# Fused attention and two MoE layers on one core: both halves of a batch's q product in one burst, and the token softmax emitted by stage for both halves

## The chip, the cores and the metric

The kernel runs on one core of a Trainium2 chip. The metric is the device time of one execution in microseconds; the kernel before takes 607.36 us in the median of three runs (606.77 to 608.14).

## The reference

Three layers follow one another on 8 batches of 576 tokens with 8 heads of 64.

```python
p_packed = sm_attn(p, k, v)            # 32 packed queries per head attend to k, v
out = sm_attn(q, p_packed, p_packed)   # the tokens attend to the packed result

# MoE 1: every token goes to the one expert with the largest logit
h = np.maximum(xe @ w1[e], 0.0)
out[mask] = gate_w[mask, None] * (h @ w2[e])

# MoE 2: only tokens with a positive skip score, the others pass through
y[mask] = gate_w[mask, None] * (h @ w2[e])
out[do_compute] = xc + y
```

## The kernel before, in words

**Tiling.** The tokens of one batch are handled in two halves of 288 columns (`hf`), over 128 partitions. The first softmax (packed queries against k) gives per batch a packed matrix `PKT` (128x128). The token softmax gives, per batch, an attention matrix `A2` (128 partitions, 2 x 576) of weights on the packed rows. Since MoE 1 multiplies attention output by `w1`, the kernel does not form the attention output: it multiplies `PKT` by the batch's `w1` once (the q product, matrix Q1 of 128 x 2 x 1024) and then Q1 by `A2`. Expert weights are chosen at run time, per batch, from a register (`e1`).

**Precision.** An f32 product that must be exact to nearly full f32 is made of three fp32r matmuls, from a high part and a remainder of each operand. `split` (L596) makes them: a copy on ScalarE gives the high part (`Q1h`, `W2h`, `A2h`), a subtraction on VectorE or GpSimd gives the rest (`Q1l`, `W2l`, `A2l`). The q product itself is a plain f32 product on a tiled array (64 rows x 32 columns, helper `heads`, L384), and the trace has 16 matmul records for one half of it, and 32 for both.

**Main stream.** `gen_M(b)` is what TensorE does for batch b: for each half of the tokens `stage1` (8 steps of 6 matmuls, L690, `h`, evacuated by ScalarE L695 to `hh` and by VectorE L696 to `hl`) and `stage2` (4 output tiles t of 24 matmuls each, L711, `y`, reading `W2h`/`W2l` of t; each is multiplied by the gate on VectorE, L731). That makes 48 steps per batch. I write M(0) to M(7) for the batches' streams. After M(7) come the expert items of MoE 2.

**Side work.** `Weave` puts steps of other generators between the 48 steps, at fractional positions given in a table (L1330 on). For batch b the sides are the tail of batch b-1 (logits, gate), the attention work A (for batch b+1: token softmax `gen_T`, for b+2: first softmax `gen_S`, then the routing `gen_R`), `gen_pre(b+1)` (load `W1c`, split `A2`, q product, split Q1, load the gate row gB) and `gen_w2(b+1)` (load the four `W2c` tiles, split them: W2h on ScalarE, W2l on GpSimd). The recorded program is then put in order engine by engine by a scheduler that goes by priorities, and `tc.issue_after` adds an edge to that order on one engine.

**The places the change touches.** `gen_T` (L505 to L544): for each half two transposes into `T` (L520), a maximum (L523), subtraction (L525), exponential on ScalarE (L528), sum (L531), reciprocal (L533, L535), product with the reciprocal on GpSimd (L536), and two transposes into `A2` (L541). On TensorE 16 matmuls read the result: `L<-A,gs` (L554). `gen_pre` (L602 to L661): the two halves n of the q product, each with its own burst on TensorE, two `Q1h` casts and two `Q1l` subtractions; the `W1c` pool has two buffers, so the second half's two loads of 512 KB wait until the first burst has read the first half's. All DMAs of this part are issued in order by one queue, SP's. A `W2h`/`W2l` tile has one buffer for each t, so the cast for the next batch waits until the current batch's `y` matmuls of that t are done; the `W2c` pool has two buffers, so the third load waits until GpSimd has split the first.

Of the kernel before, what the change touches and what calls it, by code (L numbers as in the profile page):

```python
# [9 lines left out]
F32 = mybir.dt.float32  # L10
# [109 lines left out]
def attn_moe_kernel(ctx, tc, q, k, v, p, wg, w11, w12, w21, w22, out):  # L120
# [357 lines left out]
    def gen_T(b):  # L478
# [36 lines left out]
        for hf in range(2):  # L515
            T = Tt[hf]
            Tv = T.rearrange("p x (c e) -> p (x c) e", e=32)
            with tc.issue_after(d["turned"] if hf else e1_ins) if b == 0 else nullcontext():
                for x in range(2):
                    nc.vector.transpose(out=T[:, x, :], in_=s2[hf][x][:, 0:HALF])  # L520
            yield
            mx2 = st_p.tile([128, 18], F32, name="mx2")
            nc.vector.tensor_reduce(out=mx2, in_=Tv, op=ALU.max, axis=AX.X)  # L523
            yield
            (nc.gpsimd if b == 0 and hf else nc.vector).tensor_tensor(  # L525
                out=Tv, in0=Tv, in1=mx2.unsqueeze(2).to_broadcast([128, 18, 32]), op=ALU.subtract
            )
            nc.scalar.activation(out=T, in_=T, func=ACTF.Exp, scale=0.125)  # L528
            yield
            sm2 = st_p.tile([128, 18], F32, name="sm2")  # L530
            nc.vector.tensor_reduce(out=sm2, in_=Tv, op=ALU.add, axis=AX.X)  # L531
            yield
            nc.vector.tensor_scalar(out=sm2, in0=sm2, scalar1=EPS, scalar2=None, op0=ALU.add)  # L533
            rc2 = st_p.tile([128, 18], F32, name="rc2")
            nc.vector.reciprocal(out=rc2, in_=sm2)  # L535
            (nc.gpsimd if b or hf else nc.vector).tensor_tensor(  # L536
                out=Tv, in0=Tv, in1=rc2.unsqueeze(2).to_broadcast([128, 18, 32]), op=ALU.mult
            )
            yield
            for x in range(2):  # L540
                last = nc.vector.transpose(out=A2[:, x, hf * HALF:(hf + 1) * HALF], in_=T[:, x, :]).ins  # L541
            d["turned"] = last
            yield
# [57 lines left out]
    def gen_pre(b):  # L601
# [7 lines left out]
        def lw(n):  # L609
            for z in range(2):  # L610
                if b == 0 and n:
                    w = us[0]["y"].rearrange("p t c -> p (t c)")[:, F * z:F * (z + 1)]
                    w = w.rearrange("p (h f) -> p h f", h=2)
                else:
                    w = wcp.tile([128, 2, 512], F32, tag="W1c", name="W1c")
                nc.sync.dma_start(
                    out=w,
                    in_=w11[dsn(e1, 1), n, z].rearrange("o p h f -> p (o h) f"),
                )
                W1.append(w)  # L620

        lw(0)
        if b == 0:
            lw(1)
# [12 lines left out]
        for n in range(2):  # L637
            if b or n == 0:
                cuts = halve(n)
            yield TE  # L640
            ps = [mt("q1") for _ in range(2)]
            heads(ps, PKT, lambda hp: W1[2 * n + hp // 2][:, hp % 2, :], start=True, stop=True)
            if n == 0 and b:
                lw(1)
            sl = slice(512 * n, 512 * n + 512)
            for x in range(2):
                with ExitStack() as order:
                    for ins in cuts if b == 0 and n == 0 else ():
                        order.enter_context(tc.issue_after(ins))
                    split(Q1h[:, x, sl], Q1l[:, x, sl], ps[x], nc.vector)  # L650
                yield
        if b == 0:
# [66 lines left out]
    def gen_M(b, halves=(0, 1)):  # L719
        d = us[b]  # L720
        if halves[0] == 0 and "y" not in d:
            d["y"] = bulk.tile([128, 4, S], F32, tag="y", name="y1", bufs=2)
# [587 lines left out]
    for b in range(B):  # L1310
# [19 lines left out]
        if b + 1 < B:  # L1330
# [3 lines left out]
            sides.append((pre, 7, 0.66, 0.97))  # L1334
# [55 lines left out]
        elif b == B - 1:  # L1390
            us[b]["y"] = bulk.tile([128, 4, S], F32, tag="y", name="y1", bufs=2)
# [261 lines left out]
```

## Time and profile before

| | |
|---|---|
| median of 3 runs | 607.36 us (606.77 to 608.14) |
| profiled execution, time | 607.03 us |
| its span, first to last instruction | 605.4 us (1.63 us lie around it) |
| mean granted TensorE clock | 0.997 |
| busy: TensorE | 588.2 us (97%) |
| busy: VectorE | 335.7 us (55%) |
| busy: ScalarE | 211.2 us (35%) |
| busy: GpSimd | 136.5 us (23%) |
| HBM traffic | 200 GB/s over the span |
| steady batch, start of the first stage 2 to the next | 48.74 us (94.27 to 143.01) |

A busy share of 97% does not say that the matmuls run back to back at their best rate: matmuls are pipelined, their ends are modelled, and a matmul that starts late or a change between forms of matmul is counted as busy. So the rows of TensorE are to be read by their starts: in a row of `y` matmuls one starts every 0.13 us, and each larger distance is time that something cost. The chain of waits gives, in order of time, what each stretch went to; the timeline gives starts, durations and, in square brackets, the idle time before an instruction and what ended it.

### The profile page before, as it was taken

To read this page: it belongs to the slowest core of one execution; us is meant where nothing else is said; L and a number is where in the kernel's file an instruction comes from. 1 tells how busy PE (TensorE), PEld (TensorE's weight loads), DVE (VectorE), ACT (ScalarE), POOL (GpSimd) and SP (SyncE) were. 2 spreads that over 40 slices of the span, in tenths; PEclk is the share of its full clock that TensorE was granted. 3 is DMA by queue.
4 is the path that set the end of the run, shared out by engine and by line. 5 is a ranking of instruction groups with operands and counts; after the bars stand their busy time and mean duration, and the time that the engine had idled before them with its cause. 6 is when DMAs were issued, how large, how long until landed. Compare 5 with 4: busy or idle time off the path is not lost.

```text
span 605.4 us, 14688 instructions
## 1 busy us (share of the span) xinstructions
PE 588.2 (97%) x5901; PEld 528.1 (87%) x5902; DVE 335.7 (55%) x1000; ACT 211.2 (35%) x463; POOL 136.5 (23%) x122
## 2 busy tenths in 40 slices
PE   7899999999999999999999999999999999999996
PEld 3379889899889889989989988899899999998795
DVE  3878557737737746855774873445746236162110
ACT  3463441542352343244154224215324225043110
POOL 4041331050160141133114104120300230140032
PEclk9999999999999999999999999999999999999998
DMA  8887877477477476637326314969328491732064
GB/s 321 348 324 270 324 265 257 143 284 251 154 249 271 180 241 255 245 108 292 142 104 254 143 45 149 290 188 390 134 92 306 64 375 62 217 76 88 1 98 61
DMA packets 35994, 122.00 MB, mean 202 GB/s; under 512 B 5696, under 2 KB 15680, under 8 KB 29888
## 3 DMA queue, kind: packets, MB, share of 16 engines
q1 hardware_dynamic: 30352, 114.75, 51.8%
q0 software_dynamic: 3968, 4.85, 6.3%
q10 hardware_dynamic: 1584, 1.25, 0.7%
q8 instruction: 50, 0.82, 0.6%
q14 instruction: 40, 0.33, 0.2%
HBM read 91.57 MB, written 29.26 MB: 200 GB/s over the span
## 4 chain that ended last, share of the span: by engine, by line
PE 72%; DMA 7%; another core or an unknown queue 6%; issue 4%; DVE 4%; SPq 3%; ACT 2%; POOL 1%; POOLq 0%; ACTq 0%; DVEq 0%
PE y L711 28%; PE h L690 24%; PE y L1288 8%; PE s L386 3%; PE q L386 2%; DMA out_dram<-iXR 2%; PE L L554 1%; DMA W2c<-in_w_dram 1%; DMA W1c<-in_w_dram 1%; PE L L757 1%; DMA eX<-x2d 1%; PE pv L448 1%; SPq L995 1%; PE at L435 1%
## 5 line engine op out<-in xcount | busy, mean ns | idle before, releaser
L711 PE MATMUL y<-hh,W2h 128*128 128x288 f32 x512 | 156.0, 305 | 0.5 <-ACT hh L695 0.5
L711 PE MATMUL y<-hl,W2h 128*128 128x288 f32 x512 | 151.4, 296 | 0.7 <-DVE hl L696 0.6
L711 PE MATMUL y<-hh,W2l 128*128 128x288 f32 x512 | 151.2, 295 | 0.0
L711 PEld LDWEIGHTS y<-hh,W2h 128*128 128x128 f32 x512 | 96.0, 188 | 15.9 <-issue 11.9
L711 PEld LDWEIGHTS y<-hh,W2l 128*128 128x128 f32 x512 | 96.5, 188 | 1.1 <-issue 1.1
L711 PEld LDWEIGHTS y<-hl,W2h 128*128 128x128 f32 x512 | 96.2, 188 | 1.2 <-DVE hl L696 1.2
L598 POOL TENSOR_TENSOR W2l<-W2c,W2h 128x1024 fp32r<-128x1024 f32 x28 | 67.2, 2399 | 131.3 <-ACT W2h L597 72.0
L690 PE MATMUL h<-A2h,Q1h 128*128 128x288 f32 x256 | 78.0, 305 | 1.7 <-DVE T L520 1.4
L695 ACT ACTIVATE hh<-h 128x288 fp32r<-128x288 f32 x128 | 51.6, 414 | 69.9 <-PE h L690 56.9
L690 PE MATMUL h<-A2h,Q1l 128*128 128x288 f32 x256 | 75.6, 296 | 0.1
L690 PE MATMUL h<-A2l,Q1h 128*128 128x288 f32 x256 | 75.4, 295 | 0.0
L696 DVE SCALAR_TENSOR_TENSOR hl<-h,hh 128x288 fp32r<-128x288 f32 x128 | 56.5, 452 | 28.4 <-ACT hh L695 26.7
L690 PE MATMUL h<-eXh,eW1h 128*128 128x288 f32 x192 | 57.7, 301 | 0.8 <-DMA x2d<-y 0.8
L1288 PE MATMUL y<-ihh,iW2h 128*128 128x288 f32 x192 | 56.9, 296 | 0.0
L1288 PE MATMUL y<-ihh,iW2l 128*128 128x288 f32 x192 | 56.6, 295 | 0.0
L690 PE MATMUL h<-eXl,eW1h 128*128 128x288 f32 x192 | 56.6, 295 | 0.0
L1288 PE MATMUL y<-ihl,iW2h 128*128 128x288 f32 x192 | 56.6, 295 | 0.0
L690 PE MATMUL h<-eXh,eW1l 128*128 128x288 f32 x192 | 56.6, 295 | 0.0
L690 PEld LDWEIGHTS h<-A2h,Q1h 128*128 128x128 f32 x256 | 48.0, 188 | 6.0 <-issue 2.6
L731 DVE TENSOR_TENSOR y<-y,gB 128x288 f32<-128x288 f32 x60 | 26.7, 447 | 46.8 <-PE y L711 46.8
L690 PEld LDWEIGHTS h<-A2h,Q1l 128*128 128x128 f32 x256 | 48.1, 188 | 0.5 <-DVE Q1l L598 0.3
L690 PEld LDWEIGHTS h<-A2l,Q1h 128*128 128x128 f32 x256 | 48.1, 188 | 0.0
(299 smaller groups left out, 945.3 us busy)
## 6 DMA issues: line engine op xcount, KB each, us to landing
eW<-in_w_dram SPq DMA_DIRECT2D x8, 2048.0 KB
W1c<-in_w_dram SPq DMA_DIRECT2D x30, 512.0 KB
W2c<-in_w_dram SPq DMA_DIRECT2D x30, 512.0 KB
kT<-in_k_dram SPq DMA_DIRECT2D x7, 1152.0 KB
qT<-in_q_dram SPq DMA_DIRECT2D x7, 1152.0 KB
v<-in_v_dram SPq DMA_DIRECT2D x7, 1152.0 KB
x2d<-y SPq DMA_DIRECT2D x7, 1152.0 KB
out_dram<-y SPq DMA_DIRECT2D x7, 1152.0 KB
```

What stands on the lines that cost most here:

```text
L386: m = nc.tensor.matmul(out=out[x][32 * hp:32 * hp + 32], lhsT=lhsT[64 * x:64 * x + 64, 32 * hp:32 * hp + 32], rhs=rhs(hp)[64 * x:64 * x + ...
L435: last = nc.tensor.transpose(ats[x][:, 128 * j:128 * j + 128], a1[:, x, 128 * j:128 * j + 128], ident).ins
L448: nc.tensor.matmul(out=pv[x][32 * hp:32 * hp + 32], lhsT=aT[:, 4 * x + j, 32 * hp:32 * hp + 32], rhs=vm[:, 2 * hp + x, j, :], start=(j == ...
L554: nc.tensor.matmul(out=L[32 * i:32 * i + 32, 0:LN], lhsT=gs[:, g, :], rhs=A2[:, g, c:c + LN], start=(g == 0), stop=(g == 1),)
L598: z = eng.tensor_tensor(out=lo, in0=x, in1=hi.bitcast(F32), op=ALU.subtract)
L690: nc.tensor.matmul(out=ps[:, 0:nr], lhsT=l[:, t, 128 * f:128 * f + 128], rhs=r[:, t, :], start=(n == 0), stop=(n == 3 * kt - 1),)
L695: nc.scalar.activation(out=hh[:, f, :], in_=ps[:, 0:n_], func=ACTF.Relu)
L696: nc.vector.scalar_tensor_tensor(out=hl[:, f, :], in0=ps[:, 0:n_], scalar=0.0, in1=hh[:, f, :].bitcast(F32), op0=ALU.max, op1=ALU.subtract,)
L711: nc.tensor.matmul(out=ps[:, 0:HALF], lhsT=l[:, f, :], rhs=r[:, f, :], start=(n == 0), stop=(n == 23))
L731: nc.vector.tensor_tensor(out=y1[:, t, cols], in0=ps[:, 0:HALF], in1=d["gB"][:, cols], op=ALU.mult)
L757: nc.tensor.matmul(out=L[32 * i:32 * i + 32, 0:LN], lhsT=wgB[:, t, :], rhs=y1[:, t, LC[i]:LC[i] + LN], start=(t == 0), stop=(t == 3),)
L1288: nc.tensor.matmul(out=ps[:, 0:HALF], lhsT=l[:, f, 128 * t:128 * t + 128], rhs=r[:, f, c], start=(n == 0), stop=(n == 23))
```

## The change

It has two parts.

1. **One burst.** In `gen_pre(b)` for b from 1 to 7 both halves of `W1c` are loaded at once: the second half goes into the `y` buffer of the coming batch, which nothing uses yet. Both halves of `A2` are split ahead of the product, and the 32 matmuls of both q halves are emitted together, into four PSUM banks, where the second burst stood (24 `y` matmuls before the end of the batch). The four `Q1h` casts and four `Q1l` subtractions follow together. The positions in the table change to match.
2. **By stage.** In `gen_T(b)` for b from 1 to 7 the six stages (turn, most, less, total, over, back) are emitted for half 0 and half 1 in turn, with an order edge from one stage to the next up to the fourth. Batch 0 keeps its order.

The work is the same: TensorE has the same number of instructions in both.

```diff
@@ -512,35 +512,57 @@
         A2 = pk_p.tile([128, 2, S], F32, name="A2")
         d["A2"] = A2
         yield
-        for hf in range(2):
-            T = Tt[hf]
-            Tv = T.rearrange("p x (c e) -> p (x c) e", e=32)
-            with tc.issue_after(d["turned"] if hf else e1_ins) if b == 0 else nullcontext():
-                for x in range(2):
-                    nc.vector.transpose(out=T[:, x, :], in_=s2[hf][x][:, 0:HALF])
-            yield
-            mx2 = st_p.tile([128, 18], F32, name="mx2")
-            nc.vector.tensor_reduce(out=mx2, in_=Tv, op=ALU.max, axis=AX.X)
-            yield
-            (nc.gpsimd if b == 0 and hf else nc.vector).tensor_tensor(
-                out=Tv, in0=Tv, in1=mx2.unsqueeze(2).to_broadcast([128, 18, 32]), op=ALU.subtract
-            )
-            nc.scalar.activation(out=T, in_=T, func=ACTF.Exp, scale=0.125)
-            yield
-            sm2 = st_p.tile([128, 18], F32, name="sm2")
-            nc.vector.tensor_reduce(out=sm2, in_=Tv, op=ALU.add, axis=AX.X)
-            yield
-            nc.vector.tensor_scalar(out=sm2, in0=sm2, scalar1=EPS, scalar2=None, op0=ALU.add)
-            rc2 = st_p.tile([128, 18], F32, name="rc2")
-            nc.vector.reciprocal(out=rc2, in_=sm2)
-            (nc.gpsimd if b or hf else nc.vector).tensor_tensor(
-                out=Tv, in0=Tv, in1=rc2.unsqueeze(2).to_broadcast([128, 18, 32]), op=ALU.mult
-            )
-            yield
+        mxs, sms, rcs = ([st_p.tile([128, 18], F32, name=n) for _ in range(2)] for n in ("mx2", "sm2", "rc2"))
+        Tv = [T.rearrange("p x (c e) -> p (x c) e", e=32) for T in Tt]
+
+        def wide(t):
+            return t.unsqueeze(2).to_broadcast([128, 18, 32])
+
+        def turn(hf):
             for x in range(2):
-                last = nc.vector.transpose(out=A2[:, x, hf * HALF:(hf + 1) * HALF], in_=T[:, x, :]).ins
-            d["turned"] = last
-            yield
+                ins = nc.vector.transpose(out=Tt[hf][:, x, :], in_=s2[hf][x][:, 0:HALF])
+            return ins
+
+        def most(hf):
+            return nc.vector.tensor_reduce(out=mxs[hf], in_=Tv[hf], op=ALU.max, axis=AX.X)
+
+        def less(hf):
+            eng = nc.gpsimd if b == 0 and hf else nc.vector
+            ins = eng.tensor_tensor(out=Tv[hf], in0=Tv[hf], in1=wide(mxs[hf]), op=ALU.subtract)
+            nc.scalar.activation(out=Tt[hf], in_=Tt[hf], func=ACTF.Exp, scale=0.125)
+            return ins
+
+        def total(hf):
+            return nc.vector.tensor_reduce(out=sms[hf], in_=Tv[hf], op=ALU.add, axis=AX.X)
+
+        def over(hf):
+            nc.vector.tensor_scalar(out=sms[hf], in0=sms[hf], scalar1=EPS, scalar2=None, op0=ALU.add)
+            nc.vector.reciprocal(out=rcs[hf], in_=sms[hf])
+            eng = nc.gpsimd if b or hf else nc.vector
+            return eng.tensor_tensor(out=Tv[hf], in0=Tv[hf], in1=wide(rcs[hf]), op=ALU.mult)
+
+        def back(hf):
+            for x in range(2):
+                ins = nc.vector.transpose(out=A2[:, x, hf * HALF:(hf + 1) * HALF], in_=Tt[hf][:, x, :])
+            d["turned"] = ins.ins
+            return ins
+
+        stages = (turn, most, less, total, over, back)
+        if b:
+            last = None
+            for n, stage in enumerate(stages):
+                now = []
+                for hf in range(2):
+                    with tc.issue_after(last) if last is not None and n < 4 else nullcontext():
+                        now.append(stage(hf))
+                    yield
+                last = now[1].ins
+        else:
+            for hf in range(2):
+                for n, stage in enumerate(stages):
+                    with tc.issue_after(d["turned"] if hf else e1_ins) if n == 0 else nullcontext():
+                        stage(hf)
+                    yield
         nc.sync.dma_start(out=a2d[b].rearrange("p g u c -> p g (u c)"), in_=A2)
 
     def gen_R(b):
@@ -608,8 +630,8 @@
 
         def lw(n):
             for z in range(2):
-                if b == 0 and n:
-                    w = us[0]["y"].rearrange("p t c -> p (t c)")[:, F * z:F * (z + 1)]
+                if n:
+                    w = us[b]["y"].rearrange("p t c -> p (t c)")[:, F * z:F * (z + 1)]
                     w = w.rearrange("p (h f) -> p h f", h=2)
                 else:
                     w = wcp.tile([128, 2, 512], F32, tag="W1c", name="W1c")
@@ -620,8 +642,9 @@
                 W1.append(w)
 
         lw(0)
-        if b == 0:
-            lw(1)
+        if b > 1:
+            us[b]["y"] = bulk.tile([128, 4, S], F32, tag="y", name="y1", bufs=2)
+        lw(1)
         yield
         A2 = st[b]["A2"]
         d["A2h"] = [q1p.tile([128, 2, HALF], F32R, tag=f"A2h{i}", name="A2h") for i in range(2)]
@@ -634,22 +657,32 @@
         Q1l = q1p.tile([128, 2, F], F32R, name="Q1l")
         d["Q1"] = (Q1h, Q1l)
         PKT = st[b]["PKT"]
-        for n in range(2):
-            if b or n == 0:
-                cuts = halve(n)
-            yield TE
+        def product(n):
             ps = [mt("q1") for _ in range(2)]
             heads(ps, PKT, lambda hp: W1[2 * n + hp // 2][:, hp % 2, :], start=True, stop=True)
-            if n == 0 and b:
-                lw(1)
+            return ps
+
+        def cut(n, ps, cuts=()):
             sl = slice(512 * n, 512 * n + 512)
             for x in range(2):
                 with ExitStack() as order:
-                    for ins in cuts if b == 0 and n == 0 else ():
+                    for ins in cuts:
                         order.enter_context(tc.issue_after(ins))
                     split(Q1h[:, x, sl], Q1l[:, x, sl], ps[x], nc.vector)
                 yield
-        if b == 0:
+
+        cuts = halve(0)
+        if b:
+            yield
+            halve(1)
+            yield TE
+            ps = [product(n) for n in range(2)]
+            for n in range(2):
+                yield from cut(n, ps[n])
+        else:
+            for n in range(2):
+                yield TE
+                yield from cut(n, product(n), () if n else cuts)
             halve(1)
             yield
         while "gm" not in st[b]:
@@ -718,8 +751,6 @@
 
     def gen_M(b, halves=(0, 1)):
         d = us[b]
-        if halves[0] == 0 and "y" not in d:
-            d["y"] = bulk.tile([128, 4, S], F32, tag="y", name="y1", bufs=2)
         y1 = d["y"]
         Q1h, Q1l = d["Q1"]
 
@@ -1331,7 +1362,8 @@
             pre = gen_pre(b + 1)
             w2 = gen_w2(w12, us[b + 1], False)
             sides.append((chain(part(pre, 1), part(w2, 1)), 2, 0.5, 0.6))
-            sides.append((pre, 7, 0.66, 0.97))
+            sides.append((part(pre, 2), 2, 0.7, 0.85))
+            sides.append((pre, 5, 0.88, 1.0, TE))
             sides.append((w2, 4, 0.76, 1.1))
         if b < B - 1:
             W = Weave(gen_M(b), NM, sides, EVERY if b else 2)
@@ -1388,7 +1420,6 @@
             W.add(expect("nox"), 1, 0.92, 0.92)
             W.run()
         elif b == B - 1:
-            us[b]["y"] = bulk.tile([128, 4, S], F32, tag="y", name="y1", bufs=2)
             iA = slice(0, 1)
             d0 = {}
```

The scheduler decides the final order, so the places that matter are shown as the two programs have them.

ScalarE near the end of M(2): `a` is the exponential of the first softmax, `W2h` and `Q1h` the casts for the next batch, `aT` the next step of the attention. Before:

```order
L418 ACTIVATE a_2637,sm<-s_2520,nm 128x288
L597 CAST W2h<-W2c 128x1024
L597 CAST Q1h<-q_2571 128x512
L597 CAST Q1h<-q_2572 128x512
L597 CAST W2h<-W2c 128x1024 x2
L597 CAST Q1h<-q_2671 128x512
L597 CAST Q1h<-q_2672 128x512
L597 CAST W2h<-W2c 128x1024
L438 COPY aT<-at 128x512 x2
```

With the change:

```order
L418 ACTIVATE a_2618,sm<-s_2519,nm 128x288
L619 CAST W2h<-W2c 128x1024 x3
L619 CAST Q1h<-q_2652 128x512
L619 CAST Q1h<-q_2653 128x512
L619 CAST Q1h<-q_2662 128x512
L619 CAST Q1h<-q_2663 128x512
L619 CAST W2h<-W2c 128x1024
L438 COPY aT<-at 128x512 x2
```

The two `Q1h` casts of the first half no longer stand ahead of the second `W2h` cast, and all four now stand behind the third `W2h` cast.

SyncE's queue in the second half of M(0) before, where the second-half `W1c` loads stand (`ISA` rows set the expert's address):

```order
L359 DMA pT<-in_p_dram 128x128
L359 DMA qT<-in_q_dram 128x2304
L359 DMA kT<-in_k_dram 128x2304
L616 ISA
L616 DMA W1c<-in_w_dram 128x1024
L616 ISA
L616 DMA W1c<-in_w_dram 128x1024
L593 ISA
L593 DMA W2c<-in_w_dram 128x1024
L593 ISA
```

With the change, earlier in M(0), right behind the first half's loads and the store of `A2` (`a2d`), where before the two `W2c` loads followed:

```order
L566 DMA a2d<-A_737 128x1152
L638 ISA
L638 DMA W1c<-in_w_dram 128x1024
L638 ISA
L638 DMA y_145<-in_w_dram 128x1024
L638 ISA
L638 DMA y_145<-in_w_dram 128x1024
L615 ISA
L615 DMA W2c<-in_w_dram 128x1024
```

The second half's loads moved ahead of pT, qT and kT and ahead of two `W2c` loads; their target is now the `y` buffer.

VectorE in the token softmax of M(3) before, from half 0's sum to the last transposes (`T_2911` is half 0, `T_2912` half 1):

```order
L531 TENSOR_REDUCE sm_3010<-T_2911 128x18
L525 TENSOR_TENSOR T_2912<-T_2912,mx_3051 128x576
L533 TENSOR_SCALAR sm_3010<-sm_3010 128x18
L535 RECIPROCAL rc_3021<-sm_3010 128x18
L531 TENSOR_REDUCE sm_3078<-T_2912 128x18
L541 STREAM_TRANSPOSE A_2969<-T_2911 128x288 x2
L731 TENSOR_TENSOR y_2752<-y,gB 128x288
L533 TENSOR_SCALAR sm_3078<-sm_3078 128x18
L535 RECIPROCAL rc_3088<-sm_3078 128x18
L598 TENSOR_TENSOR A2l<-A_2969,A2h 128x576
L541 STREAM_TRANSPOSE A_2969<-T_2912 128x288 x2
```

With the change (`T_2905` is half 0, `T_2906` half 1), from the second maximum:

```order
L527 TENSOR_REDUCE mx_2975<-T_2906 128x18
L531 TENSOR_TENSOR T_2905<-T_2905,mx_2974 128x576
L531 TENSOR_TENSOR T_2906<-T_2906,mx_2975 128x576
L762 TENSOR_TENSOR y_2434<-y,gB 128x288
L536 TENSOR_REDUCE sm_2976<-T_2905 128x18
L536 TENSOR_REDUCE sm_2977<-T_2906 128x18
L539 TENSOR_SCALAR sm_2976<-sm_2976 128x18
L539 TENSOR_SCALAR sm_2977<-sm_2977 128x18
L540 RECIPROCAL rc_2978<-sm_2976 128x18
L540 RECIPROCAL rc_2979<-sm_2977 128x18
L762 TENSOR_TENSOR y_2434<-y,gB 128x288
L546 STREAM_TRANSPOSE A_2963<-T_2905 128x288 x2
```

Half 1's sum, reciprocal and product no longer stand behind half 0's transposes and a `y` product; half 0's reciprocal now stands behind half 1's sum, and the split `A2l` behind half 1's transposes.

## Rows read from the trace of the kernel before

**Rows 1.** The page: the head and TensorE's busy time.

```profile
span 605.4 us, 14688 instructions
PE 588.2 (97%) x5901; PEld 528.1 (87%) x5902; DVE 335.7 (55%) x1000; ACT 211.2 (35%) x463; POOL 136.5 (23%) x122
```

**Rows 2.** Waits of TensorE: engine, line, releaser; us in total, times, longest.

```profile
PE L L554 <- DVE A L541: 0.8, 1, 0.8
```

**Rows 3.** Chain of waits, M(0) and M(1): start, us, what.

```profile
42.95 0.68 PE L L554 x16
...
68.71 7.83 DMA W1c<-in_w_dram
...
106.46 1.10 PE L L554 x16
...
126.51 3.40 PE y L711 x24
...
130.89 3.19 PE h L690 x24
```

**Rows 4.** Timeline of TensorE around M(1)'s first burst: start, us, engine, line, operation.

```profile
117.58 0.29 PE L711 MATMUL y<-hh,W2l 128*128 128x288 f32 x1
117.81 1.09 PE L386 MATMUL q<-W1c,PKT 64*32 64x512 f32 x16
118.83 0.40 PE L711 MATMUL y<-hh,W2h 128*128 128x288 f32 x1
119.07 0.30 PE L711 MATMUL y<-hl,W2h 128*128 128x288 f32 x1
```

**Rows 5.** Timeline of TensorE, the same burst cut to 117.5 to 118.2 us.

```profile
117.81 0.66 PE L386 MATMUL q<-W1c,PKT 64*32 64x512 f32 x8
```

**Rows 6.** Timeline of TensorE, M(0)'s second burst.

```profile
75.42 2.22 PE L386 MATMUL q<-W1c,PKT 64*32 64x512 f32 x16 [0.88 <-DMA W1c<-in_w_dram]
```

**Rows 7.** Timeline of SyncE's queue in M(0).

```profile
56.80 0.33 SPq L616 DMA_DIRECT2D W1c<-in_w_dram  x1
...
68.12 0.94 SPq L616 DMA_DIRECT2D W1c<-in_w_dram  x2
```

**Rows 8.** Timeline of ScalarE, first W2h cast in M(0).

```profile
67.96 1.05 ACT L597 CAST W2h<-W2c 128x1024 fp32r<-128x1024 f32 x1
```

**Rows 9.** Timeline of VectorE, token softmax in M(1).

```profile
97.66 0.70 DVE L525 TENSOR_TENSOR T<-T,mx 128x576 f32<-128x576 f32 x1
98.30 0.73 DVE L523 TENSOR_REDUCE mx<-T 128x18 f32<-128x576 f32 x1
...
101.90 0.75 DVE L531 TENSOR_REDUCE sm<-T 128x18 f32<-128x576 f32 x1 [0.42 <-ACT T L528]
...
104.39 0.76 DVE L598 TENSOR_TENSOR A2l<-A,A2h 128x576 fp32r<-128x576 f32 x1
106.20 0.84 DVE L541 STREAM_TRANSPOSE A<-T 128x288 f32<-128x288 f32 x2 [1.05 <-POOL T L536]
```

**Rows 10.** Timeline of GpSimd, the same stretch.

```profile
101.62 1.16 POOL L536 TENSOR_TENSOR T<-T,rc 128x576 f32<-128x576 f32 x1 [16.95 <-DVE rc L535]
104.52 1.65 POOL L536 TENSOR_TENSOR T<-T,rc 128x576 f32<-128x576 f32 x1 [1.74 <-DVE rc L535]
```

**Rows 11.** Timeline of VectorE in M(6).

```profile
346.99 1.53 DVE L598 TENSOR_TENSOR A2l<-A,A2h 128x576 fp32r<-128x576 f32 x1
348.45 0.82 DVE L541 STREAM_TRANSPOSE A<-T 128x288 f32<-128x288 f32 x2
```

**Rows 12.** Timeline of ScalarE, end of M(1).

```profile
125.97 1.05 ACT L597 CAST W2h<-W2c 128x1024 fp32r<-128x1024 f32 x1 [2.67 <-DMA W2c<-in_w_dram]
126.92 1.07 ACT L597 CAST Q1h<-q 128x512 fp32r<-128x512 f32 x2
```

**Rows 13.** Timeline of VectorE, end of M(1).

```profile
127.54 1.29 DVE L598 TENSOR_TENSOR Q1l<-q,Q1h 128x512 fp32r<-128x512 f32 x2 [1.55 <-ACT Q1h L597]
```

**Rows 14.** Timeline of SyncE's queue, end of M(1).

```profile
122.32 3.80 SPq L593 DMA_DIRECT2D W2c<-in_w_dram  x2
```

## The prediction

> **What bounds the kernel now.** I read the page first: TensorE is busy for 588.2 of 605.4 us [rows 1]. So the time can only fall where TensorE waits or where its matmuls start further apart than they could, and it can only rise where a new wait ends last in front of it. The list of TensorE's waits then has few and short ones, among them 0.8 us on the transposes `A` [rows 2]. That list is too short: a matmul that starts late is also counted as a long one, so I went on to the chain of waits and to TensorE's timeline and read starts there. The reader should see three things. The 16 `L` matmuls take 1.10 us in M(1), and in the chain the same row stands in M(2) to M(5), while they took 0.68 us where their input was ready [rows 3]. A burst of the q product stands in the `y` row like an island with a shore on both sides [rows 4]. In M(0) the second burst waits and is stretched by a load [rows 6].
>
> **Part 1, one burst: entering and leaving.** Before the burst a `y` starts at 117.58, after it at 118.83 and 119.07 [rows 4]. Two plain steps of 0.13 us would have taken 0.27, so the burst puts 119.07 - 117.58 - 0.27 = 1.22 us into the row. Cut to its first part, the burst has 8 records and 0.66 us; whole, 16 records and 1.09 us [rows 4, 5]: another group of 8 costs 0.43 us. A burst of 32 therefore costs 1.22 + 2 x 0.43 = 2.08, where two of 16 cost 2.44. That is 0.36 us per batch; what is saved is one entry and one exit. Its ends are 0 (if the cost belongs to each 16 matmuls and not to the change of form) and 0.36; as the modelled end of a matmul can make 0.43 a little small, I take 0.33. It happens in M(0) to M(6): 7 x 0.33 = **2.3 us**.
>
> **Part 1, the load in M(0).** The second half's `W1c` loads are issued at 68.12, behind the first burst, whose reads they wait for, and behind the loads of qT and kT [rows 7]. The wait for it lasts 7.83 us in the chain [rows 3]. The second burst then stands idle for 0.88 us and takes 2.22 us where 1.09 is usual [rows 4, 6]: 0.88 + 1.13 = 2.01 us. In the change these loads follow the first half's, which began at 56.80, so they have some 15 us before the burst, twice the 7.83. The `y` buffer that they go into was last read by GpSimd's splits of batch 0, long before. All of it goes: **2.0 us**. In the other batches no such stall stands in the chain, so earlier loads bring nothing there. Moving them past pT, qT, kT and past two `W2c` loads delays those by two transfers of 512 KB; the first of those `W2c` tiles is cast at 67.96 [rows 8], over 10 us after the first `W1c` load was issued, which hides it at no cost. Without that cover the first `W2h` cast would start late by as much, and all later casts behind it on ScalarE, the `Q1h` too.
>
> **Part 1, what queues behind what.** On ScalarE all four `Q1h` casts now stand behind the third `W2h` cast, and that one waits for a `W2c` load: issued at 122.32, the cast began at 125.97, 3.65 us later [rows 12, 14]. Behind the casts are the `Q1l` subtractions on VectorE, and `h` of the next batch waits for these. I lay it out in the times of M(1). The burst would end at 126.51 - 0.33 = 126.18 [rows 3]. The cast ends at 125.97 + 1.05 = 127.02, two `Q1h` take 1.07 more [rows 12], one more `Q1l` of 0.65 [rows 13]: 128.74 for the first half of Q1. The `h` that needs it would start at 130.89 - 0.33 = 130.56 [rows 3]. So 1.8 us are left, less perhaps 0.2 for the hand-overs: **cost 0**, hidden by the 24 `y` matmuls and the transposes of `a` behind the burst. The second half is ready 1.1 + 0.2 us later and is read from the fifth `h` step on, which has more room.
>
> **Part 2, the softmax by stage.** In M(1) the last transposes start at 106.20 and end at 107.04, while the first `L` matmul starts before 106.46 [rows 3, 9]. They wait for GpSimd's second product, from 104.52 on, and that waits for the reciprocal of half 1, which stood behind the transposes of half 0 [rows 9, 10]. Before, GpSimd's first product began at 101.62 [rows 10]. In the change half 1's sum stands ahead of it, a pass of 0.75 us [rows 9]; half 1's subtraction stood ahead of it already. So it begins at 102.4, and the second, whose reciprocal is ready by then, follows at once: 102.4 + 2 x 1.16 = 104.7 [rows 10], and with 0.84 for the transposes [rows 9] 105.6. That is 0.9 us ahead of `L`, which then takes 0.68 instead of 1.10. From M(1) to M(5): 5 x 0.42 = **2.1 us**. In M(0) both products end late because one of them starts late on GpSimd, which the stages hardly alter: 0. In M(6), where TensorE waits 0.8 us [rows 2], the transposes of half 1 come at 348.45, behind an `A2l` of 1.53 us [rows 11]; by the same working they come a microsecond earlier, but the scheduler also placed the 12 `L` matmuls seven `y` matmuls, 0.9 us, earlier. Between 0 and 0.8 I take **0.4 us**.
>
> One row here needs a second look: GpSimd's second product takes 1.65 us and the first 1.16, and VectorE's `A2l` of 0.76 us lies over its start [rows 9, 10]. If 1.65 were its own length, the transposes would end at 106.1 and still be in time; the sum is the same, but the room shrinks to 0.4 us. The Trainium skill says more (SBUF — State Buffer, Who interferes with whom): a VectorE instruction with two inputs in SBUF and a GpSimd instruction that reads SBUF take one shared port as an exclusive lock, and the later one is blocked. By that rule the 1.65 belongs to `A2l`, which the change puts behind half 1's transposes, and the room is the whole 0.9 us. The trace agrees in M(6), where `A2l` itself is the one that takes 1.53.
>
> **The sum.** 2.3 + 2.0 + 2.1 + 0.4 = 6.8 us off the profiled 607.03: 600.2. The median of the runs shown, 607.36, is 0.33 above that execution, which would give 600.6. I say **600.4 us**.
>
> **The rivals.**
>
> *A. The stages gain nothing.* VectorE works in order, and the `y` products stand between the stages, waiting for TensorE; or GpSimd stays late. Against it is the room of 0.9 us. It leaves 2.3 + 2.0: 607.03 - 4.3, about 602.8. Chance 0.15.
>
> *B. The burst saves nothing or the load in M(0) is only moved.* For it: the shores of the burst are read from modelled ends, and in M(0) the queue before the burst is full. It takes off 2.0 to 2.3: about 602.4. Chance 0.1.
>
> *C. It is given back later.* The tail from M(6) on goes through SyncE's queue (the expert loads) and three small waits of TensorE. If that queue does not come forward by the same amount, TensorE would wait at the end for what it has saved: about 607. Against it, in M(6) that queue is itself released by `y` matmuls, which come earlier. This is also what no effect looks like. Chance 0.05.
>
> *D. Slower.* The `W2c` load lands late, the third `W2h` cast with it, and four `Q1h` casts, four `Q1l` and the next batch's first `h` behind them. Before, two of the four `Q1h` were already done by then. It decides from 3.65 + 1.6 = 5.25 us from issue to cast. Should that load take the 7.83 us that the `W1c` wait of M(0) had [rows 3], each of 7 batches would lose 2.6 us: 18 us, about 618. If it is only a microsecond over the point, 7 us are lost, and it is no change. Against it: two `W1c` loads of 512 KB that ran just ahead of this load are gone, so it should land sooner. Chance 0.08. The Trainium skill has a rule that points the same way (TensorEngine Tiling (Array Packing), PSUM Bottleneck): tiling speeds up the matmuls but not the emptying of PSUM, which may become the bottleneck. Here four banks wait to be emptied at once after 2.1 us of matmuls; no run so far shows them emptied in one go.
>
> **How the numbers follow.** The forecast has 0.62. About 0.2% of the time, 1.2 us, is what a measurement of this kernel can tell from no change. A, B and the forecast are faster by more than that, D is slower, C is no change; a mild D falls between. So **0.87** faster, **0.05** no change, **0.08** slower. The range: the lower end takes 0.36 for each burst, 0.8 in M(6) and a microsecond for small waits behind these, about 599.0. The upper end takes in A and B, and A and B together with a part missing, to 604.0. Outside lie D, C and little else.
>
> **What would show it.** In the changed profile: a row of q x32 in each of M(0) to M(6) that puts 2.1 us between `y` matmuls; no wait on `W1c`; the batch's period, 48.74, shorter by 0.75 us; `L` x16 at 0.68 in M(1) to M(5), with the last transposes ending before 106.1 in M(1)'s old times; `A2l` and the products on GpSimd without stretch. I would be wrong if `h` of a new batch waits on `Q1l` or `Q1h`, if the third `W2h` cast starts more than 1.6 us after the burst's end, or if TensorE's waits from M(7) on grow.

## The result, and the profile after

| | before | with the change |
|---|---|---|
| median (runs) | 607.5 us (4; 606.77 to 608.14) | 601.51 us (4; 600.74 to 602.77) |
| ratio | | 0.9895, interval 0.9866 to 0.9925 |
| profiled execution | 607.03 us, span 605.4 | 600.74 us, span 599.0 |
| steady batch | 48.74 us | 47.95 us (92.63 to 140.58) |

The changed kernel is 6.0 us faster. I had said 600.4 us, between 599.0 and 604.0, so it came out as forecast. Run a second time beside other kernels it took 600.72 us (6 runs, 599.55 to 603.29) where the kernel before took 607.24, a ratio of 0.9886 (0.9842 to 0.9929).

The page after, its head and TensorE's busy time (compare [rows 1]):

```profile
span 599.0 us, 14675 instructions
PE 583.3 (97%) x5901; PEld 529.1 (88%) x5902; DVE 335.9 (56%) x1000; ACT 211.1 (35%) x463; POOL 134.7 (22%) x122
```

TensorE has the same 5901 matmul records and is busy for 4.9 us less: most of the gain was counted as work before. The chain of waits of the kernel after, M(0) and M(1) (start, us, what):

```profile
74.27 1.88 PE q L386 x32
76.15 3.39 PE y L744 x24
...
104.82 0.68 PE L L576 x16
...
128.47 3.19 PE h L723 x24
```

There is one burst of 32 now, no load in this stretch of the chain, and `L` takes 0.68 us where [rows 3] had 1.10. The burst in TensorE's timeline, M(1) (compare [rows 4]):

```profile
121.92 0.29 PE L744 MATMUL y<-hh,W2l 128*128 128x288 f32 x1
122.14 1.09 PE L386 MATMUL q<-W1c,PKT 64*32 64x512 f32 x16
123.03 1.06 PE L386 MATMUL q<-y,PKT 64*32 64x512 f32 x16
124.02 0.40 PE L744 MATMUL y<-hh,W2h 128*128 128x288 f32 x1
124.26 0.29 PE L744 MATMUL y<-hl,W2h 128*128 128x288 f32 x1
```

It puts 124.26 - 121.92 - 0.27 = 2.07 us into the `y` row. Two bursts of 1.22 put 2.44, so 0.37 is saved. SyncE's queue in M(0) (compare [rows 7]): the second half's loads begin at 58.17, behind the first half's.

```profile
57.62 0.33 SPq L638 DMA_DIRECT2D W1c<-in_w_dram  x1
58.17 1.92 SPq L638 DMA_DIRECT2D y<-in_w_dram  x2
```

GpSimd's products in the token softmax of M(1) (compare [rows 10]):

```profile
100.27 2.28 POOL L542 TENSOR_TENSOR T<-T,rc 128x576 f32<-128x576 f32 x2 [17.24 <-DVE rc L540]
```

VectorE behind them (compare [rows 9]):

```profile
102.58 0.84 DVE L546 STREAM_TRANSPOSE A<-T 128x288 f32<-128x288 f32 x2 [0.28 <-POOL T L542]
103.34 0.72 DVE L620 TENSOR_TENSOR A2l<-A,A2h 128x576 fp32r<-128x576 f32 x1
```

The two products follow each other without stretch, 1.14 us each, the transposes end at 103.42, and the `L` matmuls begin at 104.75: 1.3 us of room.

TensorE's waits after:

```profile
PE s L386 <- DMA pT<-in_p_dram: 2.9, 2, 1.8
...
PE L L576 <- DVE A L546: 0.3, 1, 0.3
```

The wait on `A` in M(6) fell from 0.8 to 0.3 us [rows 2]. The wait on pT stands in the first 20 us, in code that is the same in both.

**Where the 6.4 us of span went.** Taking the starts of the same rows in both chains: M(0), from the start of its 72 `y` matmuls (45.07 before, 45.80 after) to M(1)'s 84 (94.27 and 92.63), is 49.20 before and 46.83 after, 2.37 less. Each of M(1) to M(4) is 0.79 less. M(5) and the first half of M(6) (289.21 to 355.21, and 284.42 to 349.08) are 1.34 less together; the second half of M(6) to the second group of `y` of M(7) (387.41 and 380.92) 0.36 less. What lies ahead of M(0) took 0.73 us more in this execution, and what lies behind 0.1 more. The 0.73 is no part of the change: in this execution TensorE's granted clock was 0.96 over the first 45 us where it was 1.00 before, and the 32 `s` matmuls at 18.34 us took 2.42 us where the kernel before shows 1.18 (at 18.76). In the changed kernel's second profiled execution (`e11_after_again`) the same 72 `y` matmuls begin at 45.32, and in `e7_q1h_first`, which has both parts of the change, at 45.03.

### The profile page after: what moved, and what is told of

Same layout as the page of the kernel before. It is cut to its first block, busy times and chain, and to the rows that moved or that the text cites. A ratio compares the mean times of both kernels' runs of the same rounds, so it can differ in the third digit from the quotient of the medians.

```text
span 599.0 us, 14675 instructions
## 1 busy us (share of the span) xinstructions
PE 583.3 (97%) x5901; PEld 529.1 (88%) x5902; DVE 335.9 (56%) x1000; ACT 211.1 (35%) x463; POOL 134.7 (22%) x122
## 4 chain that ended last, share of the span: by engine, by line
PE 76%; DMA 7%; another core or an unknown queue 6%; issue 3%; DVE 2%; SPq 2%; ACT 2%; POOL 1%; POOLq 0%; DVEq 0%; ACTq 0%
PE y L744 31%; PE h L723 24%; PE y L1319 8%; PE s L386 3%; PE q L386 3%; DMA eW<-in_w_dram 2%; DMA pT<-in_p_dram 2%; DMA out_dram<-iXR 2%; SPq L1026 1%; PE L L788 1%; PE L L576 1%; PE pv L448 1%; PE at L435 1%; DVE eW1l L620 1%
```

## The experiments

The programs are compared with runs of the kernel before on the same chip in the same set; the ratio is to these. The edits are shown against the changed kernel, those of `e2_stages_only`, `e3_loads_only` and `e6_A2l_late` against the kernel before; `...` marks what is left out.

### The parts alone

**One burst alone** (`e1_burst_only`): the changed `gen_pre`, with the token softmax of the kernel before.

```diff
-        stages = (turn, most, less, total, over, back)
-        if b:
-            last = None
...
+        for hf in range(2):
+            T = Tt[hf]
+            Tv = T.rearrange("p x (c e) -> p (x c) e", e=32)
...
```

Expected:

> The one burst and its early loads, with the old token softmax. My theory (one burst saves 7 x 0.33, the load in M(0) 2.0 us): 4.3 us under the kernel before, ratio 0.993; L x16 stays at 1.10 us in M(1) to M(5), the TensorE wait of 0.8 us on A in M(6) stays. If instead the stages carry the gain: less than 2 us under before. If part of the burst's gain came only because the softmax is earlier (the two parts lean on each other): less than 3.5 us.

Measured: 602.49 us against 606.57, ratio 0.9931 (0.9909 to 0.9953), 4.2 us less by the ratio. A steady batch takes 48.37 us (92.04 to 140.41), 0.37 less. Its chain, M(1):

```profile
104.23 1.11 PE L L554 x16
```

`L` is late as before. The 4.3 us of bursts and load stand by themselves.

**The stages alone** (`e2_stages_only`): the staged `gen_T`, with the two bursts and late loads of the kernel before.

```diff
-        for hf in range(2):
-            T = Tt[hf]
...
+        stages = (turn, most, less, total, over, back)
+        if b:
+            last = None
+            for n, stage in enumerate(stages):
...
```

Expected:

> The staged token softmax alone, two bursts and late loads as before. My theory: 5 x 0.42 and 0.4 in M(6), 2.5 us under the kernel before, ratio 0.996; q stays as two bursts of 16, the wait on W1c in M(0) stays with 0.9 us idle. Rival: earlier transposes only move the wait to another place, under 0.5 us.

Measured: 604.53 us against 606.57, ratio 0.9961 (0.9935 to 0.9988), 2.4 us less. A steady batch takes 48.31 us (95.39 to 143.70), 0.43 less, and `L` in M(1) takes 0.68:

```profile
107.58 0.68 PE L L576 x16
```

The ratios of the two parts multiply to 0.9892; the change has 0.9895. They do not lean on each other. TensorE's second burst in M(0) of this execution:

```profile
76.53 2.25 PE L386 MATMUL q<-W1c,PKT 64*32 64x512 f32 x16 [0.24 <-DMA W1c<-in_w_dram]
```

Idle and stretched part make 0.24 + 1.16 = 1.40 us here, where the kernel before showed 2.01 [rows 6]. So the price of that load is not the same in every execution; in `e6_A2l_late`, further down, it was 2.21 + 1.69 = 3.9. Each is a single execution of another kernel.

**The early load alone** (`e3_loads_only`): both halves of `W1c` loaded at once, the two bursts at their old places.

```diff
-                if b == 0 and n:
-                    w = us[0]["y"].rearrange("p t c -> p (t c)")[:, F * z:F * (z + 1)]
+                if n:
+                    w = us[b]["y"].rearrange("p t c -> p (t c)")[:, F * z:F * (z + 1)]
...
         lw(0)
-        if b == 0:
-            lw(1)
+        if b > 1:
+            us[b]["y"] = bulk.tile([128, 4, S], F32, tag="y", name="y1", bufs=2)
+        lw(1)
...
-            if n == 0 and b:
-                lw(1)
...
```

Expected:

> Only the early load of the second half of W1c into the y buffer; the two bursts stay apart at their old places, the softmax is the old one. My theory: 2.0 us under the kernel before, all of it in M(0), ratio 0.9967; a steady batch keeps 48.74 us. Rival (the stall in M(0) only moves to another load, or the early loads help in every batch): 0 us, or over 3 us with a shorter steady batch.

Measured: 605.95 us against 606.57, ratio 0.9987 (0.9967 to 1.0007): by the runs alone the 2.0 us are not confirmed, and they are not excluded. The 12 runs spread from 604.25 to 610.39. The trace tells more. TensorE's second burst in M(0):

```profile
73.29 1.09 PE L386 MATMUL q<-y,PKT 64*32 64x512 f32 x16
```

It neither waits nor is stretched, M(0) takes 47.12 us (45.36 to 92.48) instead of 49.20, 2.08 less, and a steady batch keeps its 48.7 (92.48 to 141.20 is 48.72). Up to the expert part the gain is as expected. In the profiled execution (608.1 us) 2.7 us are lost again behind 540 us, in the expert items, which the edit does not touch: there the chain has one stretch of 39.19 us where the kernel before has 36.54, and TensorE waits:

```profile
PE pk L1132 <- DVE ecu L1128: 1.9, 1, 1.9
```

Why this part is slower in some executions stays open.

### What the one burst saves

**A gap of 6 matmuls** (`e4_split`):

```diff
-            ps = [product(n) for n in range(2)]
+            ps = [product(0)]
+            yield
+            ps.append(product(1))
...
-            sides.append((pre, 5, 0.88, 1.0, TE))
+            sides.append((pre, 6, 0.88, 1.0, TE))
```

Expected:

> The changed kernel with 6 y matmuls put between the two halves of the burst, nothing else. If what the one burst saves is one entry and one exit of the other form of matmul: 7 x 0.35 = 2.4 us over the changed kernel, and a steady batch of 48.3 us. If it saves something that hangs on the first burst's place (the Q1 casts, the third W2h cast): under 0.5 us over the changed kernel.

Measured: 603.30 us against 606.57, ratio 0.9938 (0.9915 to 0.996). That is 0.0043 above the changed kernel's first ratio, 2.6 us, and a steady batch takes 48.31 us (92.78 to 141.09), 0.36 more. The split burst in TensorE's timeline:

```profile
122.07 0.29 PE L746 MATMUL y<-hh,W2l 128*128 128x288 f32 x1
122.29 1.09 PE L386 MATMUL q<-W1c,PKT 64*32 64x512 f32 x16
123.31 0.40 PE L746 MATMUL y<-hh,W2h 128*128 128x288 f32 x1
...
124.31 1.09 PE L386 MATMUL q<-y,PKT 64*32 64x512 f32 x16
```

Both bursts have their shores again, with the loads, the casts and the softmax of the changed kernel. What is saved is the entry and the exit, 0.36 us, and nothing that hangs on the first burst's place.

**Another junction** (`e8_joined`): in M(0) to M(5) the 16 `L` matmuls directly ahead of the 32 `s` matmuls.

```diff
-    def gen_S(b):
+    def gen_S(b, join=None):
...
+        for _ in range(5 * (join is not None)):
+            yield
         yield TE
+        if join is not None:
+            next(join)
...
-        yield TE
+        if b + 1 == B:
+            yield TE
         L = mt("L")
...
-                yield from merge(PAT[1], S=gen_S(b + 1), R=gen_R(b))
+                r = gen_R(b)
+                yield from merge("SSSSSSS" + PAT[1], S=gen_S(b + 1, r), R=r)
...
-    NS, NT, NR = 5, 14, 20
+    NS, NT, NR = 5, 14, 23
...
```

Expected:

> The changed kernel with one more junction of the same kind: the 16 L matmuls are put directly ahead of the 32 s matmuls in M(0) to M(5), 42 h matmuls later than they were (the routing that follows them is late by 5.8 us). If leaving the y or h row and coming back has a price per island: an exit and an entry less in 6 batches, 6 x 0.3 = 1.8 us, and 0.5 us of the L wait in M(0), 2 us under the changed kernel. If a change between the two tiled forms (128x32 and 64x32) costs as much as one to the full array: half of that or nothing. If the late routing delays the first softmax and with it the casts: slower.

Measured: 605.88 us against 607.43, ratio 0.998 (0.9961 to 0.9998), some 5 us slower than the changed kernel by the ratios. The junction itself, TensorE's timeline:

```profile
109.79 0.29 PE L729 MATMUL h<-A2h,Q1l 128*128 128x288 f32 x1
110.01 0.75 PE L581 MATMUL L<-A,gs 128*32 128x160 f32 x16
110.69 1.20 PE L386 MATMUL s<-kT,pT 64*32 64x288 f32 x32
111.82 0.41 PE L750 MATMUL y<-hh,W2h 128*128 128x288 f32 x1
112.06 0.30 PE L750 MATMUL y<-hl,W2h 128*128 128x288 f32 x1
```

It puts 112.06 - 109.79 - 0.27 = 2.00 us into the row. In the changed kernel the two islands put 105.67 - 104.52 - 0.27 = 0.88 and 112.59 - 111.00 - 0.27 = 1.32. So 0.20 us is saved, a little over half of what a junction of two bursts of one form gives, and a steady batch shows it: 47.73 us (140.04 to 187.77) against 47.95. In M(0), where I had expected 0.5 us more, nothing is gained: it takes 46.90 us (45.40 to 92.30), the changed kernel 46.83. The steps behind the junction moved a little with it (the transposes of `a` stand 6 `y` matmuls earlier). The time is lost again in the expert part, in the same way as in `e5_late` and `e9_late_but_last` below: a wait of 4.45 us at its first `h`, and 15.36 us for the 96 `h` that took 12.88.

### Whether the casts need their cover

**The burst 18 `y` matmuls later** (`e5_late`):

```diff
-            yield TE
+            yield
             ps = [product(n) for n in range(2)]
...
-            sides.append((pre, 5, 0.88, 1.0, TE))
+            sides.append((pre, 5, 0.97, 1.0))
```

Expected:

> The changed kernel with its burst put 6 y matmuls before the end of the batch instead of 24 (18 x 0.13 = 2.4 us of cover taken away). In the changed kernel's trace of M(1) the Q1l that the next batch's first h needs ends at 126.75 and that h starts at 128.22: 1.47 us of room. My theory: h then waits about 2.4 - 1.5 = 0.9 us in 6 or 7 batches, 5 to 6 us over the changed kernel, a TensorE wait on Q1h or Q1l in the list, a steady batch of 48.9 us instead of 47.95. Rival (the casts follow the burst so fast that the cover was never needed): no change.

Measured: 606.49 us against 607.43, ratio 0.9979 (0.996 to 0.9997), 5 us above the changed kernel as I had expected, and not for my reason. A steady batch takes 47.93 us (91.92 to 139.85), as short as in the changed kernel, and no `h` from M(0) to M(6) waits for `Q1h` or `Q1l` (the list's 1.1 us on `Q1h` is batch 0's, at 26.59 us, ahead of M(0)). To see why, first the changed kernel, end of M(1): SyncE's queue,

```profile
120.24 2.70 SPq L615 DMA_DIRECT2D W2c<-in_w_dram  x2
```

ScalarE (compare [rows 12]),

```profile
123.92 1.05 ACT L619 CAST W2h<-W2c 128x1024 fp32r<-128x1024 f32 x1 [3.90 <-DMA W2c<-in_w_dram]
124.87 2.04 ACT L619 CAST Q1h<-q 128x512 fp32r<-128x512 f32 x4
```

and VectorE (compare [rows 13]):

```profile
125.48 2.48 DVE L620 TENSOR_TENSOR Q1l<-q,Q1h 128x512 fp32r<-128x512 f32 x4 [2.77 <-ACT Q1h L619]
```

The casts of Q1 begin when the third `W2h` cast ends, and that was released by the `W2c` load, 3.68 us after its issue. The burst had begun 2.7 us before. With the late burst ScalarE shows:

```profile
123.23 1.05 ACT L619 CAST W2h<-W2c 128x1024 fp32r<-128x1024 f32 x1 [3.92 <-DMA W2c<-in_w_dram]
125.01 2.05 ACT L619 CAST Q1h<-q 128x512 fp32r<-128x512 f32 x4 [0.73 <-PE q L386]
```

Now the burst releases the casts, but against the end of the batch they are only 0.9 us later (2.49 us ahead of the first `h` instead of 3.35), not 2.4, and the room takes it up. The cover of 24 `y` matmuls hides a load and not the burst.

The 5 us went elsewhere. The late kernel's list of TensorE's waits begins with

```profile
PE h L723 <- DMA gm2d<-xgT: 4.4, 1, 4.4
```

at the first `h` of the expert part, at 423.52 us, and the 96 `h` behind it take 15.12 us instead of 12.88.

**The same, but not in M(6)** (`e9_late_but_last`):

```diff
-            yield TE
+            yield TE if b == B - 1 else None
...
-            sides.append((pre, 5, 0.88, 1.0, TE))
+            sides.append((pre, 5, 0.88, 1.0, TE) if b == B - 2 else (pre, 5, 0.97, 1.0))
```

Expected:

> The late burst (6 y matmuls before the end) in M(0) to M(5) only; M(6), and so the code in front of the expert part, as in the changed kernel. The late burst in all batches kept a steady batch of 47.93 us and lost its time in one wait of 4.4 us and a slower stretch behind it in the expert part. If the 18 y matmuls of cover were not needed: within 1 us of the changed kernel, no wait over 2 us behind M(7). If the cover is needed after all and the wait was its late form: 3 us or more over the changed kernel.

Measured: 604.09 us against 607.24, ratio 0.9939 (0.9913 to 0.9966), some 3 us above the changed kernel in the same set, so the number sides with "needed after all". The trace doesn't: a steady batch takes 47.93 us (91.85 to 139.78) and nothing waits up to M(7). The loss is again one wait, in TensorE's timeline:

```profile
422.09 0.58 PE L723 MATMUL h<-eXh,eW1h 128*128 128x288 f32 x1 [3.30 <-DMA out_dram<-y]
```

The stage table of the same kernel for 418 to 436 us (columns: window, length, then busy time and records of TensorE, its weight loads, VectorE, ScalarE, GpSimd; granted clock; DMA share, GB/s):

```profile
418.00:424.00 6.00, 2.70 (x20) 2.31 (x17) 3.60 (x17) 1.51 (x3) 0.00 (x0) 0.79 0.60 212
424.00:436.00 12.00, 12.00 (x90) 12.00 (x88) 6.62 (x9) 5.30 (x10) 5.77 (x2) 0.96 0.01 3
```

and of the changed kernel, run beside it (`e11_after_again`):

```profile
418.00:424.00 6.00, 5.29 (x47) 4.88 (x46) 3.67 (x17) 0.64 (x2) 0.00 (x0) 1.00 0.67 241
424.00:436.00 12.00, 12.00 (x95) 11.45 (x93) 8.41 (x20) 6.64 (x13) 5.79 (x2) 1.00 0.01 3
```

The wait costs twice: 2.6 us more of idle time (3.30 against 0.71), and behind it matmuls at a lower granted clock, 0.79 and 0.96 instead of 1.00, so that the 96 `h` take 14.18 us instead of 12.88. It stands behind a branch of the program (the test on whether the expert part has tokens). In the DMA view of 415 to 424.2 us `e9_late_but_last` has

```profile
q8 instruction: 2, 0.03, 1.3%
```

and the changed kernel beside it

```profile
q8 instruction: 1, 0.02, 0.6%
```

`e5_late` and `e8_joined` have two such packets there as well, `e7_q1h_first` and `e10_burst_A2l`, whose first `h` waits only 1.0 and 0.9 us, one. Over the whole execution these three kernels have 51 packets on that queue, and every other kernel here has 50. That points to code that is loaded late behind the branch, which no run shows directly; the releaser that the timeline names is a store that ends at about the same time. What makes it late in these three kernels and not in the others isn't settled.

**Q1 ahead of the third W2h** (`e7_q1h_first`):

```diff
-                    split(Q1h[:, x, sl], Q1l[:, x, sl], ps[x], nc.vector)
+                    d["Q1cast"] = split(Q1h[:, x, sl], Q1l[:, x, sl], ps[x], nc.vector)[0]
...
-            split(W2h, W2l, W[t], nc.vector if early and t < 2 else nc.gpsimd)
+            with tc.issue_after(d["Q1cast"]) if t == 2 and not early else nullcontext():
+                split(W2h, W2l, W[t], nc.vector if early and t < 2 else nc.gpsimd)
```

Expected:

> The changed kernel with an order edge on ScalarE: the third W2h cast behind the Q1h casts instead of ahead of them, so that Q1h no longer queues behind the W2c load. My theory: that queue costs nothing while 1.5 us of room are left; within 0.6 us of the changed kernel, ratio to before 0.9885 to 0.990. Rival D in its mild form (it costs something in some batches): over 1 us faster than the changed kernel. Or the third W2h cast, now 1 us later, delays the fourth W2c load and the y matmuls: over 1 us slower.

Measured: 600.33 us against 607.43, ratio 0.9889 (0.987 to 0.9909), the same as the changed kernel (0.9895 and 0.9886). The queue behind the load costs nothing here, as forecast; the way out of rival D, had it been needed, is this edge.

### What made `L` late

**One order edge** (`e6_A2l_late`): the kernel before, with `A2l` of half 0 behind half 1's transposes.

```diff
         def halve(hf):
-            return split(d["A2h"][hf], d["A2l"][hf], A2[:, :, hf * HALF:(hf + 1) * HALF], nc.vector)
+            x = A2[:, :, hf * HALF:(hf + 1) * HALF]
+            a = nc.scalar.copy(out=d["A2h"][hf], in_=x)
+            with tc.issue_after(st[b]["turned"]) if b and not hf else nullcontext():
+                z = nc.vector.tensor_tensor(out=d["A2l"][hf], in0=x, in1=d["A2h"][hf].bitcast(F32), op=ALU.subtract)
+            return a.ins, z.ins
```

Expected:

> The kernel before with one order edge: A2l of half 0 behind the last transposes of half 1, on VectorE; no stages, two bursts. Two causes were named for the late transposes, the late reciprocal of half 1 and GpSimd's product stretched from 1.16 to 1.65 us by A2l. If the stretch is the larger part: the product takes 1.16, the transposes end at 106.55 instead of 107.04, L x16 falls from 1.10 to about 0.70, 2 us under the kernel before. If the late reciprocal alone carries it: L x16 stays above 1.0 us, no gain.

Measured: 606.60 us against 607.43, ratio 0.9979 (0.9953 to 1.0005), unclear by the runs, which spread from 603.69 to 610.40. The trace is plain. GpSimd's second product in M(1):

```profile
107.21 1.16 POOL L536 TENSOR_TENSOR T<-T,rc 128x576 f32<-128x576 f32 x1 [1.74 <-DVE rc L535]
```

TensorE:

```profile
109.09 0.75 PE L554 MATMUL L<-A,gs 128*32 128x160 f32 x16
```

The product takes 1.16 us, the reciprocal is as late as it was (the same 1.74 us of idle time in front as in [rows 10]), and `L` is in time, with no room left: the transposes are shown to end at 109.25. A steady batch takes 48.31 us (96.98 to 145.29), exactly what the stages give. So taking away the stretch by `A2l`, 0.49 us, is enough to take away the lateness that TensorE felt; whether the earlier reciprocal alone would be enough, no run shows, since the stages move `A2l` too. This is what the rule of the Trainium skill says (SBUF — State Buffer, Who interferes with whom), and the trace now agrees from both sides: with `A2l` beside the product 1.65, without it 1.16. A product held up to the end of `A2l` (104.39 + 0.76) would have lost 0.63 us, so the size agrees only roughly.

That the runs don't show the gain has a reason in the profiled execution: it is lost again in M(0), where the load of the second burst came later than in the kernel before.

```profile
76.55 2.78 PE L386 MATMUL q<-W1c,PKT 64*32 64x512 f32 x16 [2.21 <-DMA W1c<-in_w_dram]
```

The 25 `y` matmuls behind it, in the chain of this kernel and of the kernel before:

```profile
79.33 4.55 PE y L715 x25
```

```profile
77.65 3.53 PE y L711 x25
```

The granted clock from 76 to 85 us was 0.81 here, where the kernel before had 1.00 from 75 to 83. M(0) takes 52.11 us (44.87 to 96.98) instead of 49.20, which is more than the edge gives back in M(1) to M(5).

**The burst with that edge** (`e10_burst_A2l`): the changed `gen_pre` with the old softmax and the edge above.

Expected:

> The one burst of the change with the old token softmax and, in place of the stages, the one order edge: A2l of half 0 behind the last transposes of half 1. If the stretch of GpSimd's product by A2l is what made L late: L x16 at 0.68 in M(1) to M(5), a steady batch of 47.95, within 0.6 us of the changed kernel (the 0.4 us of M(6) are lacking). If the stages do something else as well: over 1 us above the changed kernel.

Measured: 600.47 us against 607.24, ratio 0.9877 (0.9835 to 0.9919); the changed kernel beside it (`e11_after_again`) 600.72, ratio 0.9886. Steady batches of 47.94 us (92.27 to 140.21), `L` at 0.68. One edge does what the stages do in M(1) to M(5). In M(6) it doesn't: there TensorE's wait on `A` is 0.7 us, against 0.3 in the changed kernel, a difference too small for the runs to tell.

> The changed kernel itself, for comparison within the same set of runs: 0.9895 of the kernel before, as measured.

No kernel tried was clearly faster than the changed one.

## Why the prediction was right

- **The bursts.** Forecast 0.33 us for each of 7 batches; measured 0.37 in the timeline and 0.36 by splitting the burst again. The step that it is an entry and an exit is shown by `e4_split`. The term was 2.3 and is 2.5 us.
- **The load in M(0).** Forecast 2.0. M(0) is shorter by 2.37, of which 0.36 belongs to the burst: 2.01. With the load alone M(0) is shorter by 2.08. The size is that of one execution: in two others with late loads it was 1.40 and 3.9, so it was partly luck that the one execution that I had read gave a price that held.
- **The softmax.** Forecast 0.42 in each of M(1) to M(5); measured 0.43 (`e2_stages_only`). The size was right and the way only in part. I wrote that the second product "waits for the reciprocal of half 1, which stood behind the transposes of half 0", and gave the stretch by `A2l` a second look that changed only the room. The edge alone shows that removing the stretch is enough, with the reciprocal as late as before. The room came out as 1.3 us, I had 0.9: passes of VectorE follow each other faster than their shown lengths (0.64 us from 97.66 to 98.30, shown with 0.70 [rows 9]), and a wait of 0.28 us on a `y` product, at 99.30 in the kernel before, was gone.
- **M(6).** Forecast 0.4; the wait fell by 0.47.
- **The queue on ScalarE.** Forecast no cost with 1.6 to 1.8 us of room, and the load 3.65 us after its issue; it took 3.68, and no `h` of a later batch waited for it (the 0.7 us on `Q1h` in the list of the kernel after is batch 0's, at 26.92 us). The four banks were emptied by four casts in 2.04 us and four subtractions in 2.48 us, before the first `h` began. I named the 24 `y` matmuls as the cover; `e5_late` shows that 6 would do for the batches: the burst then releases the casts, but only 0.9 us later than the load did. That step of the working was too simple, at no harm to the number.
- **The sum.** 6.8 us forecast; 2.5 + 2.0 + 2.1 + 0.5 = 7.1 by the trace, of which the profiled execution lost 0.73 ahead of M(0).
- **The rivals.** A and B fell with `e1_burst_only`, `e2_stages_only`, `e4_split` and the trace of `e3_loads_only`. D did not occur. C, that time is given back in the tail, did not occur in the change (of its signs, the wait of the expert part's first `h` was 1.1 us in this execution, 0.8 before and 0.7 in `e11_after_again`); but in `e5_late`, `e8_joined` and `e9_late_but_last` it did, by a wait that I hadn't thought of.

## What to carry to other kernels

A group of matmuls of another tiled form inside a long row costs its entry and exit once for each island, here 0.36 us, and the list of waits does not show it: read the starts on both sides of the island, and join islands where the data allow. Where two engines are slow together, look first at which operations lie over each other; here moving one subtraction behind the pair gave as much in a steady batch as rewriting the order of the whole softmax. And before you count on cover, see which releaser comes last: a burst ahead of a late load is not what the casts wait for.

## What the runs showed of the hardware that I had not expected

Between two tiled forms (128x32 and 64x32) the change costs less than leaving the full array and coming back: a junction saved 0.20 us, against 0.36 for two bursts of the same form. And small edits, in two of the three kernels all of them 100 us and more ahead of a branch, went with a longer wait behind it, 3.3 to 4.5 us where the changed kernel shows 0.7 and 1.1, with one packet more on the instruction queue and a granted clock of 0.79 to 0.83 in the 6 us around it (1.00 is the upper level, 2.4 GHz). Such a loss is larger than any term of this change.
